# Zero-padded queries, DMA transposes of token-order q and k, W_tok copies moved to ScalarE and a longer lag of the channel product, in an attention-and-mixing kernel

**Chip, cores, metric.** One core of one Trainium2 chip. The metric is device time in microseconds (us), median over executions. A run is called slow when it took over 1.5% more than the fastest run of the same kernel; a profile is called slow when it was taken in such a run. Engines in the profile: PE (TensorE matmuls), PEld (its weight loads), DVE (VectorE), ACT (ScalarE), POOL (GpSimd), SP (SyncE, which here only issues DMAs).

## The reference

```python
# q, k, v: 4 batches, 8 heads, 768 tokens, 64; n_global = 8, n_local = 96
scores = q @ k^T / 8 + ALiBi bias; only the 8 first keys and the last 96 are kept
x = (softmax(scores) @ v), heads side by side          # 4 x 768 x 512
theta = x @ w_theta
y = w_tok_r @ (x * cos(theta)) + w_tok_i @ (x * sin(theta))   # over tokens
u = x + y
out = u + relu(u @ w_ch)
```

The inputs are drawn with a factor of 0.1, so scores are close to 0: a kernel that uses another batch's q or k stays within the tolerance of the comparison, one that uses another batch's v does not.

## The kernel before

Batch 0 is attended first; after that each batch's token mixing on PE is woven with the attention of the next. `b` is the batch, `p` a pair of heads. Four parts matter.

Loads go through GpSimd, in a layout where each partition holds six consecutive tokens (long runs), so that a copy on DVE and six PE transposes per operand are needed to get q and k transposed in token order:

```python
def load_qk(b, h0, n, which=(0, 1)):
    for i_ in which:
        nc.gpsimd.dma_start(out=qk[:, i_, h0:h0 + n].rearrange("p h t d -> p h (t d)"),
            in_=(q, k)[i_][b, h0:h0 + n].rearrange("h (p t) d -> p h (t d)", p=T))

def prep(b, p, w=0):
    ...
    with behind("dve"):            # L189: reorder, q and k
        for i_ in range(2):
            (nc.scalar.copy if b == 0 and i_ and p < 2 else nc.vector.tensor_copy)(
                out=qkn[:, :, i_]..., in_=qk[:, i_, 2 * p:2 * p + 2])
    for i_, dst in ((0, qT), (1, kT)):
        for t_ in range(NT):       # L198
            nc.tensor.transpose(ps[:, t_, :], qkn[:, t_, i_]..., ident)
        if i_ == 0:
            nc.vector.tensor_copy(out=dst, in_=src)      # L203
        else:
            nc.scalar.copy(out=dst, in_=src)             # L205
    nc.vector.tensor_copy(out=kG, in_=kT[...])           # L209
    nc.vector.tensor_copy(out=kG[:, :, 0:NG], in_=...)   # L210
```

The scores of the two heads of a pair are matmuls of 64 rows each (L230, `R = slice(D * hh, D * (hh + 1))`). The transposes of x (theta needs them) and, from batch 1 on, of u (the channel product needs them) are DMA transposes issued by SyncE:

```python
def xtrans(b, p, ...):   # L292
    nc.sync.dma_start_transpose(out=xT_sb[b][:, p, :]..., in_=x_sb[b][:, p]...)
def utrans(b, tt):
    nc.sync.dma_start_transpose(out=uT, in_=u)
def chan(b, tt):         # L357: the channel product, `lag` tiles behind the mixing
    nc.tensor.matmul(ps_c, lhsT=uT[:, dc, :], rhs=w_ch_bf[:, dc, :], ...)
```

And the order of a batch:

```python
for b in range(B):
    if b + 2 < B:
        load_all(b + 2)
    lag = 2
    ...   # rest of the channel products, prep of b + 1, theta of b
    ...   # mixing of b (and channel products) woven with attention of b + 1
```

The softmax here doesn't subtract the row's maximum and nothing guards it: scores larger than these inputs give would overflow.

## Time and profile before

| | before |
|---|---|
| median (3 runs) | 191.09 us (190.76 to 193.43) |
| profiled span | 189.6 us |
| PE busy | 89% of the span |
| DVE, ACT, POOL busy | 73%, 54%, 14% |

The first theta matmul of each batch is a mark. It cuts the run into stages: from theta of batch 0 to theta of 1 (the mixing of 0, the preparation of 1, the attention of 1), theta of 1 to theta of 2, theta of 2 to theta of 3, and the rest. The next lines are the kernel before, cut there: length, then busy time and count of PE, PEld, DVE, ACT, POOL; granted clock; DMA share; GB/s.

```profile
29.50:76.70 47.20, 44.31 (x465) 25.52 (x474) 38.74 (x87) 29.92 (x37) 6.49 (x4) 1.00 1.73 153
76.70:118.50 41.80, 38.02 (x337) 18.95 (x340) 31.01 (x66) 23.24 (x26) 1.75 (x2) 0.96 0.90 133
118.50:156.80 38.30, 36.69 (x339) 18.77 (x344) 31.45 (x67) 22.74 (x25) 0.00 (x0) 1.00 0.37 80
156.80:189.60 32.80, 27.63 (x127) 11.99 (x127) 14.05 (x26) 6.56 (x7) 0.00 (x0) 1.00 0.32 97
```

PE is busy for all but 3 us of the first stage and 4 us of the second. Stages two and three have the same work on PE; the second is 3.5 us longer, and its clock of 0.96 points to the reason: PE stood for a late uT and ran at half clock for a while afterwards (the prediction shows the wait).

### The profile page before, as it was taken

The page shows a single profiled execution, that of the slowest core. Times are in us where ns is not written, and L with a number is a line of the kernel's source. Part 1 is how long each engine was busy: PE and PEld are TensorE (multiplying, and loading weights), DVE is VectorE, ACT ScalarE, POOL GpSimd, SP SyncE. Part 2 cuts the span into 40 slices and gives each one's busy share as a digit, 9 for nine tenths or more (in the row PEclk, how much of TensorE's full clock was granted, in tenths as well). Part 3 has the DMA queues.
Part 4 walks back from the last instruction along what each step waited for, and adds up shares of the span by engine and source line. Part 5 has one row for each costly group of instructions (what it writes and reads, how often), then busy time and mean ns, then how long its engine had stood idle before and what let it go on. Part 6 is the DMA issues. An engine that isn't in the chain of part 4 may idle for free.

```text
span 189.6 us, 3693 instructions
## 1 busy us (share of the span) xinstructions
PE 167.9 (89%) x1500; PEld 89.1 (47%) x1523; DVE 137.9 (73%) x309; ACT 102.9 (54%) x122; POOL 27.1 (14%) x31
## 2 busy tenths in 40 slices
PE   7855787899999999999939999999999999999981
PEld 2424665445656555654414454644454544434430
DVE  5839987386999997998853786998877864734422
ACT  2469988871397684598724360499663604800010
POOL 7974361300040004020000000000000000000000
PEclk9999669999999999999987999999999999999999
DMA  4999999999999983999991337301165374113432
GB/s 63 153 188 181 210 209 207 204 189 142 130 83 182 225 116 75 148 142 146 223 116 58 74 91 185 109 3 55 28 66 141 88 145 148 59 32 107 118 106 111
DMA packets 58081, 23.97 MB, mean 126 GB/s; under 512 B 44240, under 2 KB 54992, under 8 KB 58064
## 3 DMA queue, kind: packets, MB, share of 16 engines
q0 software_dynamic: 35760, 12.85, 70.6%
q1 hardware_dynamic: 22304, 10.88, 25.0%
q8 instruction: 12, 0.20, 0.5%
q14 instruction: 5, 0.04, 0.1%
HBM read 25.69 MB, written 6.29 MB: 169 GB/s over the span
## 4 chain that ended last, share of the span: by engine, by line
PE 55%; ACT 14%; DVE 13%; DMA 12%; issue 2%; POOL 2%; ACTq 0%; POOLq 0%
PE ps L332 22%; PE ps L357 10%; DMA uT<-u 8%; PE pb L313 7%; ACT e L234 6%; PE pb L230 5%; DMA vn<-in_v_dram 4%; PE pb L278 4%; DVE qT L203 4%; ACT cs L317 3%; PE ps L198 3%; DVE qkn L189 2%; PE ps L278 2%; DVE zri L321 2%; POOL qk L72 2%
## 5 line engine op out<-in xcount | busy, mean ns | idle before, releaser
L234 ACT ACTIVATE e<-pb 128x1024 bf16<-128x1024 f32 (+1 forms) x48 | 44.1, 958 | 25.8 <-PE pb L230 25.7
L332 PE MATMUL ps<-zri,w_tokT_111 128*128 128x512 bf16 x141 | 53.6, 381 | 0.9 <-issue 0.3
L332 PE MATMUL ps<-zri,w_tokT_110 128*128 128x512 bf16 x130 | 49.5, 382 | 1.3 <-DVE zri L321 0.8
L337 DVE TENSOR_TENSOR u<-x_sb,ps 128x512 bf16<-128x512 bf16 x24 | 16.5, 687 | 16.6 <-PE ps L332 16.0
L357 PE MATMUL ps<-w_ch_bf,uT 128*128 128x512 bf16 x94 | 25.3, 391 | 3.7 <-DMA uT<-u 3.5
L360 DVE SCALAR_TENSOR_TENSOR o_sb<-ps,u 128x512 f32<-128x512 f32 x24 | 16.5, 687 | 11.4 <-PE ps L357 11.4
L313 PE MATMUL pb<-w_theta_bf,xT 128*128 128x512 bf16 x93 | 23.6, 379 | 0.7 <-ACT xT L299 0.4
L321 DVE TENSOR_TENSOR zri<-x_sb,cs 128x512 bf16<-128x512 bf16 x48 | 18.3, 421 | 7.2 <-ACT cs L317 6.1
L242 DVE TENSOR_TENSOR e<-e,etab 128x1024 bf16<-128x1024 bf16 (+1 forms) x32 | 19.7, 617 | 3.5 <-ACT e L234 3.5
L230 PE MATMUL pb<-qT,kT 64*128 64x128 bf16 x224 | 17.9, 231 | 4.7 <-ACT e L234 4.6
L332 PEld LDWEIGHTS <-w_tokT_110 128*128 128x128 bf16 x144 | 14.1, 98 | 15.2 <-issue 1.1
L332 PEld LDWEIGHTS <-w_tokT_111 128*128 128x128 bf16 x144 | 14.1, 98 | 13.2 <-issue 0.5
L205 ACT COPY kT<-ps 128x768 bf16<-128x768 bf16 x16 | 12.9, 805 | 13.4 <-PE ps L198 13.4
L230 PEld LDWEIGHTS <-kT 64*128 64x128 bf16 x224 | 10.0, 99 | 18.3 <-issue 16.7
L351 ACT COPY uT<-ps 128x512 bf16<-128x512 bf16 x7 | 4.1, 587 | 26.1 <-PE ps L350 26.1
L317 ACT ACTIVATE cs<-pb,halfpi 128x1024 bf16<-128x1024 f32 x12 | 13.4, 1120 | 8.9 <-issue 6.8
L278 PEld LDWEIGHTS <-e 128*128 128x128 bf16 x352 | 14.7, 100 | 6.8 <-issue 1.0
L198 PE MATMUL ps<-ident,qkn 128*128 128x128 bf16 x192 | 16.1, 232 | 1.1 <-DVE qkn L189 0.9
L198 PEld LDWEIGHTS <-qkn 128*128 128x128 bf16 x192 | 12.8, 103 | 8.4 <-DVE qkn L189 6.1
L230 PE MATMUL pb<-qT,kG 64*128 64x128 bf16 x128 | 13.6, 228 | 2.0 <-DVE kG L210 2.0
L203 DVE COPY qT<-ps 128x768 bf16<-128x768 bf16 x16 | 15.2, 947 | 0.0
L357 PEld LDWEIGHTS <-uT 128*128 128x128 bf16 x96 | 8.4, 99 | 13.5 <-DMA uT<-u 4.7
(63 smaller groups left out, 204.3 us busy)
## 6 DMA issues: line engine op xcount, KB each, us to landing
out_dram<-o_sb SPq DMA_DIRECT2D x24, 256.0 KB, 2.3
qk<-in_q_dram POOLq DMA_DIRECT2D x3, 768.0 KB, 8.1
qk<-in_k_dram POOLq DMA_DIRECT2D x3, 768.0 KB, 13.6
vn<-in_v_dram POOLq DMA_DIRECT2D x3, 768.0 KB, 22.7
w_nat<-in_moe_w_tok_r_dram POOLq DMA_DIRECT2D x3, 384.0 KB, 13.6
w_nat<-in_moe_w_tok_i_dram POOLq DMA_DIRECT2D x3, 384.0 KB, 14.8
qk<-in_q_dram POOLq DMA_DIRECT2D x4, 192.0 KB, 6.4
qk<-in_k_dram POOLq DMA_DIRECT2D x4, 192.0 KB, 6.7
```

What stands on the lines that cost most here:

```text
L198: nc.tensor.transpose(ps[:, t_, :], qkn[:, t_, i_].rearrange("p h d -> p (h d)"), ident)
L203: nc.vector.tensor_copy(out=dst, in_=src)
L230: nc.tensor.matmul(pb[:, hh, o:o + T], lhsT=lhsT, rhs=qT[R, (own, nxt)[part]], start=True, stop=True)
L234: ins = nc.scalar.activation(e_c, pb[:, :, 0:n], AF.Exp, scale=scale).ins
L242: nc.vector.tensor_mul(e_c, e_c, tab[:, :, s0:s0 + n // T].rearrange("p a s n -> p a (s n)"))
L278: nc.tensor.matmul(o, lhsT=l_, rhs=r_, start=(i_ == 0), stop=(i_ == len(mms) - 1))
L313: nc.tensor.matmul(pb[:, j, :], lhsT=xT[:, dc, st * T:(st + 1) * T], rhs=w_theta_bf[:, dc, :], start=(dc == 0), stop=(dc == NC - 1))
L317: nc.scalar.activation(cs[:, 0], pb, AF.Sin, bias=halfpi)
L321: nc.vector.tensor_mul(zri[b][:, i_, 2 * c + j_, :].rearrange("p (g d) -> p g d", g=NP), xb[:, :, 2 * c + j_, :], cs[:, i_, j_].rearrange( ...
L332: anchor["pe"] = nc.tensor.matmul(ps, lhsT=w_tokT[wi][:, st, tt * T:(tt + 1) * T], rhs=zri[b][:, wi, st, :], start=(st == 0 and wi == 0), ...
L337: anchor["dve"] = nc.vector.tensor_add(u_sb[b, tt].rearrange("p (g d) -> p g d", g=NP), x_sb[b][:, :, tt, :], ps.rearrange("p (g d) -> p g ...
L357: nc.tensor.matmul(ps_c, lhsT=uT[:, dc, :], rhs=w_ch_bf[:, dc, :], start=(dc == 0), stop=(dc == NC - 1))
```

## The change

The intent: PE and DVE are full, the DMA engines and GpSimd are not. So (1) q and k of batches 2 and 3 are loaded in token order and transposed by DMA, which frees 48 PE transposes and some 16 copies a batch; (2) since such a transpose brings two heads or a head and zeros at once, q is kept zero-padded (`qZ`: 128 rows, the other head's are 0), and the scores of batches 1 to 3 use all 128 rows; (3) SyncE's order is fixed to the program's; (4) W_tok copies go from DVE to ScalarE; (5) the channel product comes three tiles behind the mixing instead of two in batches 1 to 3. The small constants move into other buffers to make room.

```diff
+    def load_qk_nat(b):
+        if b == 2:
+            for a in range(2):
+                nc.gpsimd.memset(q_nat[:, a::2, :, 1 - a, :], 0.0)
+        for h in range(H):
+            for i_, dst in ((0, q_nat[:, h, :, h % 2, :]), (1, k_nat[:, h // 2, :, h % 2, :])):
+                nc.gpsimd.dma_start(out=dst, in_=(q, k)[i_][b, h].rearrange("(t p) d -> p t d", p=T))
...
-            (copy if wi else nc.vector.tensor_copy)(out=w_tokT[wi][:, :, tt * T:(tt + 1) * T], in_=ps)
+            nc.scalar.copy(out=w_tokT[wi][:, :, tt * T:(tt + 1) * T], in_=ps)
...
+        if b > 1:
+            with behind("pe"):
+                for dst, src in ((kT, k_nat[:, p]), (qT[:, 0], q_nat[:, 2 * p]), (qT[:, 1], q_nat[:, 2 * p + 1])):
+                    nc.sync.dma_start_transpose(out=..., in_=...)
+            return
...
+            if i_ == 0 and b:
+                for hh, copy in ((0, nc.scalar.copy), (1, nc.vector.tensor_copy)):
+                    R = slice(D * hh, D * (hh + 1))
+                    copy(out=dst[R, hh]..., in_=src[R])
+                continue
...
-                    R = slice(D * hh, D * (hh + 1))
+                    R = slice(0, T) if b else slice(D * hh, D * (hh + 1))
...
-        lag = 2
+            lag = 3 if b else 2
...
-            order = rest[:-1] + pre[:2] + th[:2] + pre[2:] + th[2:3] + rest[-1:] + th[3:]
+            order = pre + rest[:-1] + th[:3] + rest[-1:] + th[3:] + keys[:1]
```

(`keys[:1]` is the kG copy of the first pair. The natural buffer `home` shares its space with batch 1's run layout, so batch 2's q waits for batch 1's reorder copies, and each load of batch 3 for the transpose that frees its part. Cut: buffers, constants, SyncE's manual order.)

## The prediction

> **What bounds the kernel now.** I read the page's slices first, then the busy time of each engine by stage, then the chain of waits, then single lines. The slices show TensorE (PE) nearly full from slice 8 on; slice 21 (99.5 to 104.3 us) is the only late one with a lowered clock.
>
> ```profile
> PE   7855787899999999999939999999999999999981
> PEclk9999669999999999999987999999999999999999
> DMA  4999999999999983999991337301165374113432
> ```
>
> I cut the time after batch 0's attention where the chain changes from mixing (L332) to the transposes and theta (L198, L313) and back. Columns: length, then busy time and count of PE, weight loads, DVE, ACT, GpSimd (POOL), clock, DMA.
>
> ```profile
> 42.00:75.40 33.40, 32.41 (x366) 19.17 (x373) 29.77 (x64) 19.54 (x24) 4.17 (x3) 1.00 1.92 136
> 75.40:88.00 12.60, 12.50 (x103) 6.58 (x104) 12.31 (x34) 9.56 (x12) 1.86 (x3) 1.00 1.38 141
> 88.00:118.80 30.80, 27.13 (x248) 13.10 (x252) 20.30 (x36) 13.77 (x15) 0.00 (x0) 0.94 0.69 131
> 118.80:130.00 11.20, 10.97 (x90) 5.91 (x91) 11.09 (x31) 8.80 (x10) 0.00 (x0) 1.00 0.19 61
> 130.00:155.30 25.30, 24.27 (x245) 12.46 (x248) 19.37 (x34) 13.94 (x16) 0.00 (x0) 1.00 0.42 82
> ```
>
> I call them B (mixing of batch 0 beside attention of 1), C (theta of 1, preparation of 2), D (mixing of 1, attention of 2), E and F (the same one batch on), G the rest. In B and in C and E, DVE is as full as PE; D and F are PE's own. D is 5.5 us longer than F with the same work, and the chain says why: a transposed u came late behind the loads of batch 3.
>
> ```profile
> 90.08 8.61 DMA uT<-u
> 98.69 0.05 issue
> 98.74 1.89 PE ps L357 x4
> ```
>
> PE stood 3.1 us (95.6 to 98.7), and the 3.4 us after that ran at a granted clock of 0.54, so about 1.6 us more were lost.
>
> Durations that I need, from the groups by form and the per-tile view:
>
> ```profile
> L205 ACT COPY kT<-ps 128x768 bf16<-128x768 bf16 x16 | 12.9, 805 | 13.4 <-PE ps L198 13.4
> L203 DVE COPY qT<-ps 128x768 bf16<-128x768 bf16 x16 | 15.2, 947 | 0.0
> L162 DVE COPY w_tokT_110<-ps 128x768 bf16<-128x768 bf16 x6 | 3.3, 554 | 2.4 <-PE ps L161 2.4
> L292 SPq DMA_TRANSPOSE xT<-x_sb x12: 1209/1214/1889, 63.1 to 154.4; - x12
> DMA to landing us min/median/max: 2.7/2.8/6.3
> 83.39 0.85 PE ps L198 x12
> 125.96 0.69 PE ps L198 x12
> ```
>
> PE's true pitch is in the last two: 12 transposes in 0.69 us, 57.5 ns each, when nothing holds them.
>
> The score matmuls, from the timeline of PE (start, busy time):
>
> ```profile
> 102.63 0.19 PE L278 MATMUL pb<-vG,e 128*128 128x65 bf16 x1
> 102.76 0.23 PE L230 MATMUL pb<-qT,kT 64*128 64x128 bf16 x2
> 102.83 0.22 PE L230 MATMUL pb<-qT,kG 64*128 64x128 bf16 x2
> ...
> 102.94 0.22 PE L230 MATMUL pb<-qT,kG 64*128 64x128 bf16 x2
> 103.09 0.39 PE L332 MATMUL ps<-zri,w_tokT_110 128*128 128x512 bf16 x1
> ```
>
> **What the Trainium skill says.** (1) "TensorE: Matmul & The Clock Gate", Part 1: a warm matmul of 128 columns starts every 55.6 ns, one of 512 every 215.7 ns, and an idle array falls to half clock. The trace agrees: 57.5 ns, 0.216 us from one L332 start to the next, and the 0.54 clock after the gap. (2) "TensorEngine Tiling (Array Packing)", Key Properties: a change of tiling mode drains the array. The trace agrees: the eight 64-row score matmuls that begin at 102.76 follow each other by 57 ns per pair of heads, but 0.10 us is lost before them and 0.09 us after them; 0.43 us in all. (3) "DMA: Bandwidth & Descriptors", Queues, rings and completion order: each DMA engine goes round its queues a packet at a time. So a load and a transpose share: the same uT transpose lands 2.4 us after issue at the median and 8.6 us at worst, in the load of batch 3.
>
> **Zero-padded scores.** Batches 1 to 3 use all 128 rows, one matmul per head: a group of 8 costs 8 x 57.5 ns = 0.46 us against 0.43 with the drains; a group of 6, 0.35 against 0.37. A batch has 8 groups of 8 and 4 of 6: +0.2 us a batch. That is a wash, not a gain. What it buys is that the transposed DMA of zero-filled q needs no shuffle.
>
> **Transposes by DMA (batches 2, 3).** C and E each lose 48 PE transposes (48 x 57.5 ns = 2.8 us), 8 qkn copies on DVE (8 x 0.35 = 2.8), 4 qT copies (3.8) and, on ACT, 4 kT copies (3.2). Added on SyncE: 12 transposes of 128x768 at 1.21 us of issue, 14.5 us a batch. The theta stage does not shrink by all 2.8: six Sin of about 1.07 us (6.4) and a table load (1.28) follow the first theta in series. With two chans and four theta pieces ahead of it the first Sin begins some 3.5 us in, as it does now; I take 0.8 us of new PE idling. So -2.0 for each of C and E.
>
> Does the data arrive? Natural-order loads are runs of 64 instead of 384 elements. From the DMA table in 58 to 62 us the long runs went at 266 packets/us, so q and k of one batch (2048) take 7.7 us; v's short ones (79 to 81) at 1134 per us, so 12288 would take 10.8. GpSimd's issue was 0.73 us for 2 rows per partition and 1.46 for 24: about 0.85 us for 6, so 16 issues take 13.6 us. For batch 2, k needs no buffer of the run layout and comes early; q must wait for the qkn copies (L189, to 54 us) and should land by about 70, before the transposes at about 76. Good.
>
> For batch 2 the transposes run from the end of B, beside v of batch 3 (6144 short packets, 5.4 us) and then k and q of batch 3, which follow pair by pair as the transposes release the natural buffer. Work for the DMA engines from there: 12 x 0.93 us (768 packets at some 830 per us, an estimate from the transposes at 116 to 118 us) + 5.4 + 10.8 = 27 us; so the last pair may come 26 us after the start, and SyncE's fixed order puts the uT of D behind it. The first chan of D wants its uT about 24 us after the start (lag is now 3 tiles). I put a loss of 2.7 us between 0 and 5.5. For batch 3 no load runs and 14.5 us of issue fits before the uT is wanted.
>
> **D and F otherwise.** The 3.1 us stand and 1.6 us half-clock of D go: -4.7, with +2.7 new and +0.2 for padding. F: +0.2. The longer lag moves one chan out of D into E and one out of F into G, which is no gain in itself.
>
> **B.** Ten W_tok copies leave DVE there (10 x 0.55 = -5.5 us) and go to ACT at 0.8 (the duration of its copies from PSUM), +8. The q eviction of batch 1 is now two half copies, each still 768 elements long (L259 on 128 partitions takes 0.70 us and L260 on 8 takes 0.69, so partitions do not count): DVE keeps 4 x 0.95, ACT gains 4 x 0.8 = 3.2. ACT goes from 19.5 to 30.7 us in a stage of 33.4. Its exponentials can start only after q, k and W_tok copies, 2 to 4 us later than the present 54.2. PE's work does not shrink in B. I take +1.8. The zero fills on GpSimd sit behind a DMA backlog that lasts to 53 us, so cost nothing.
>
> **G.** The wait of 0.7 us for a uT of batch 2 (PE at 155.2 to 155.95) goes: -0.7. The 1.2 us hole at 182.5, before the last u's transposes, stays, since PE's built order still has those transposes ahead of the last chans.
>
> Sum: B +1.8, C -2.0, D -1.8, E -2.0, F +0.2, G -0.7 = -4.5, giving 186.6. My D figure may be harsh, since the lag was lengthened for exactly this wait and the DVE relief in B is real; I take 1.4 us off for that and say 185.2.
>
> **Rivals.** *DMA takes over in D.* If transposes are served only after the natural loads, the first uT comes 5 to 8 us late, PE falls to half clock again and D gains nothing: 189 to 191. For it: the 8.6 us landing, and each load now in four times as many packets. Against: the loads of batch 3 themselves wait for the transposes, so cannot run ahead. *ACT becomes B's bound.* 30.7 busy of 33.4 with waits between gives +4: 187.5. For it: ACT row above; against: back-to-back ACT copies start 0.7 us apart, not 0.8. *All hidden.* Transposes finish under theta and mixing; B unchanged: 180 to 181. For it: DMA is under half used after 100 us.
>
> **Range and chances.** The first two rivals add, the third takes off as much: 180 to 190.5. Faster by over 2% is below 187.3, with the centre 2 us under it: 0.68. Within 2%: 0.28. Slower than 194.9 needs both bad rivals at once: 0.04.
>
> **What would show it.** Right: no L198 work after B, C about 10.5 us, ACT above 28 us in B with the first exponential at 56 to 58, D's wait on uT no longer than 5 us, kT and qZ transposes of the second preparation at 2.8 us landing and the first at 5 or more. Wrong: an idle PE of over 5 us waiting for uT or qZ in D, a DVE that waits for kT with the zri products behind it, or B longer than 38 us. If D falls by 6 us or more the DMA sharing was far milder than I took.

## The result

| | before | after |
|---|---|---|
| median | 192.2 us (4 runs, 190.76 to 193.43) | 206.28 us (4 runs, 204.49 to 208.65) |
| profiled span | 189.6 | 206.6 (a slow run) |
| PE, DVE, ACT, POOL busy | 89, 73, 54, 14% | 84, 64, 52, 28% |

The changed kernel is slower: ratio 1.065, 95% interval 1.049 to 1.082. A ratio here and below is the mean time of one kernel's fast runs over that of the other's of the same rounds, so not quite the ratio of the quoted medians. The profiled run of after was one of its slow ones; its fast runs were 204.5 and 204.9 us. So I read only waits from it that a fast profile of a variant shows too (the variant of experiment 1 has the same ones, most of them shorter, at 204.5 us of span).

The slices of after (40 of 5.2 us), to set against those in the prediction:

```profile
PE   6856878899669999983899289979997998999982
PEclk9999589999757999997599969999999999999998
DMA  5999999999999137599999992777788567305424
```

PE has holes at slices 10, 18 and 22 (52, 93 and 114 us), each with a lowered clock at or after it, and DMA is full from slice 17 to 23 and at 0.7 to 0.8 from 25 to 30, where before it was mostly at 0.3 or less from slice 21 on. By stage, after:

```profile
30.00:85.30 55.30, 49.15 (x467) 30.24 (x464) 40.08 (x75) 39.98 (x51) 21.31 (x21) 0.91 1.49 131
85.30:135.20 49.90, 39.56 (x300) 21.13 (x298) 26.92 (x54) 20.74 (x22) 13.69 (x17) 0.90 1.48 146
135.20:173.40 38.20, 35.21 (x297) 19.17 (x296) 26.57 (x55) 19.84 (x21) 0.00 (x0) 1.00 0.73 152
173.40:206.60 33.20, 27.76 (x129) 12.06 (x127) 14.12 (x27) 6.56 (x7) 0.00 (x0) 0.97 0.37 102
```

Of the 17 us between the two profiles, 8.1 are in the first stage, where POOL works 21.3 us instead of 6.5, and 8.1 in the second. About 4 of the 17 belong to the slow run (208.65 against 204.5 and 204.9); in which stage they fell is not known. The third, without its 48 PE transposes, is only 0.1 us shorter, though PE's busy time there is 1.5 us less and DVE's 4.9. PE's waits in it (in all, times, longest), which before had one of 0.4 us for a uT:

```profile
PE pb L354 <- DMA xT<-x_sb: 1.4, 1, 1.4
PE ps L398 <- DMA uT<-u: 1.2, 1, 1.2
```

**The first stage.** One of DVE's copies in the kernel before (start, busy time); then DVE's timeline of after, and GpSimd's over the same time:

```profile
49.93 0.17 DVE L210 COPY kG<-kT 128x32 bf16<-128x32 bf16 x1
```

```profile
51.31 2.10 DVE L207 COPY kG<-kT 128x32 bf16<-128x32 bf16 x1
55.25 2.73 DVE L207 COPY kG<-kT 128x32 bf16<-128x32 bf16 x1
```

```profile
51.22 2.21 POOL L90 DMA_DIRECT2D vn<-in_v_dram  x1
...
54.87 1.70 POOL L86 DMA_DIRECT2D home<-in_q_dram  x2
56.55 1.40 POOL L83 MEMSET home<- 128x1536 bf16 x1
```

A copy of 32 columns took 0.17 us in the kernel before; here one takes 2.10 and ends at 53.41 us with GpSimd's issue of v (53.43), another 2.73, beside two issues of q and a zero fill, and ends at 57.98 just after the fill (57.95; GpSimd's ends are rough in this profile). The Trainium skill has the mechanism, in "SBUF — State Buffer", Who interferes with whom: DVE in a two-port mode (which copies can enter if their operands allow it) and GpSimd share a pair of ports under an exclusive lock, and the second to come blocks wholly. The trace agrees by the ends above; the experiments test it. This is what I did not think of. Why GpSimd is busy then: in before, v of batch 2 was issued at 32.5 us, long before; in after its issue (51.2) stands behind the keys' eight small loads, the last five of which wait for earlier transfers to land.

**The second stage.** DVE's timeline of after (in brackets: idle before, and what ended it), then the chain of waits:

```profile
85.23 0.69 DVE L401 SCALAR_TENSOR_TENSOR o_sb<-ps,u 128x512 f32<-128x512 f32 x1 [0.18 <-PE ps L398]
94.72 0.29 DVE L206 COPY kG<-kT 128x512 bf16<-128x512 bf16 x1 [8.80 <-DMA kT<-home]
95.13 0.76 DVE L362 TENSOR_TENSOR zri<-x_sb,cs 128x512 bf16<-128x512 bf16 x2
```

```profile
88.75 10.17 DMA qZ<-home
...
110.69 8.62 DMA uT<-u
119.31 0.05 issue
119.36 1.71 PE ps L398 x4
```

DVE stood 8.8 us for the first transposed keys of batch 2, with the zri products that the mixing of batch 1 needs queued behind; then the uT of the channel product took 8.6 us, behind the 12 transposes and beside the loads of batch 3. The 8.6 us that bounded this stage in before are still there, though the product is wanted a tile later, and the 8.8 are new. GpSimd issues loads in this stage too, but they hold DVE little: no kG copy there takes over 0.58 us.

### The profile page after: what moved, and what is told of

Read it like the earlier page. It is cut to its first block, busy times and chain, and to the rows that moved or that the text cites.

```text
span 206.6 us, 3598 instructions
## 1 busy us (share of the span) xinstructions
PE 173.5 (84%) x1427; PEld 96.4 (47%) x1427; DVE 132.5 (64%) x274; ACT 107.8 (52%) x129; POOL 58.7 (28%) x69
## 4 chain that ended last, share of the span: by engine, by line
PE 47%; DVE 20%; DMA 17%; ACT 7%; SPq 4%; issue 2%; POOL 1%; ACTq 0%; POOLq 0%
PE ps L373 23%; PE ps L398 7%; PE pb L272 6%; DMA uT<-u 6%; DMA qZ<-home 5%; DMA vn<-in_v_dram 4%; PE pb L354 3%; PE pb L319 3%; DVE kG L207 3%; DVE e L283 2%; ACT cs L358 2%; ACT e L275 2%; DVE e L286 2%; DVE zri L362 2%; POOL home L76 1%
## 5 line engine op out<-in xcount | busy, mean ns | idle before, releaser
L373 PE MATMUL ps<-zri,w_tokT 128*128 128x512 bf16 x288 | 77.4, 394 | 5.4 <-DVE zri L362 5.3
L275 ACT ACTIVATE e<-pb 128x1024 bf16<-128x1024 f32 (+1 forms) x48 | 44.3, 959 | 31.5 <-PE pb L272 31.5
L373 PEld LDWEIGHTS <-w_tokT 128*128 128x128 bf16 x288 | 26.9, 101 | 30.9 <-issue 8.8
L272 PEld LDWEIGHTS <-kT 128*128 128x128 bf16 (+1 forms) x224 | 17.4, 106 | 15.4 <-issue 11.3
L272 PE MATMUL pb<-qZ,kT 128*128 128x128 bf16 x168 | 19.7, 232 | 0.9 <-DMA qZ<-home 0.5
L86 POOL DMA_DIRECT2D home<-in_k_dram x16 | 13.3, 836 | 23.0 <-DMA kT<-home 9.5
L86 POOL DMA_DIRECT2D home<-in_q_dram x16 | 13.6, 858 | 8.0 <-DMA qZ<-home 7.7
L354 PEld LDWEIGHTS <-xT 128*128 128x128 bf16 x96 | 8.8, 98 | 14.8 <-DMA xT<-x_sb 4.4
L90 POOL DMA_DIRECT2D vn<-in_v_dram x5 | 9.6, 1923 | 20.5 <-DVE rec L327 20.4
L272 PE MATMUL pb<-qZ,kG 128*128 128x128 bf16 x96 | 13.6, 232 | 0.2 <-DVE kG L207 0.2
L319 PE MATMUL pb<-vn,e 128*128 128x65 bf16 x168 | 12.3, 193 | 0.6 <-DVE e L286 0.4
## 6 DMA issues: line engine op xcount, KB each, us to landing
w_nat<-in_moe_w_tok_i_dram POOLq DMA_DIRECT2D x3, 384.0 KB, 14.3
```

The lines of the kernel that those rows point to most:

```text
L86: nc.gpsimd.dma_start(out=dst, in_=(q, k)[i_][b, h].rearrange("(t p) d -> p t d", p=T))
L272: nc.tensor.matmul(pb[:, hh, o:o + T], lhsT=lhsT, rhs=rhs, start=True, stop=True)
L275: ins = nc.scalar.activation(e_c, pb[:, :, 0:n], AF.Exp, scale=scale).ins
L319: nc.tensor.matmul(o, lhsT=l_, rhs=r_, start=(i_ == 0), stop=(i_ == len(mms) - 1))
L354: nc.tensor.matmul(pb[:, j, :], lhsT=xT[:, dc, st * T:(st + 1) * T], rhs=w_theta_bf[:, dc, :], start=(dc == 0), stop=(dc == NC - 1))
L373: anchor["pe"] = nc.tensor.matmul(ps, lhsT=w_tokT[wi][:, st, tt * T:(tt + 1) * T], rhs=zri[b][:, wi, st, :], start=(st == 0 and wi == 0), ...
```

## The experiments

All times below are medians; "stages" are the four lengths between the theta marks in the one profile of that run. The jobs ran on different chips, each with its own runs of before; in the job of 9 to 12 two runs of before took 326 us, for a reason not known, and count as slow.

| kernel | us | ratio to before | stages |
|---|---|---|---|
| before | 191.8 to 192.5 | 1 | 47.2, 41.8, 38.3, 32.8 |
| after (slow profile) | 206.28 | 1.065 | 55.3, 49.9, 38.2, 33.2 |
| 1 after, W_tok on DVE | 207.47 | 1.078 | 51.2, 49.2, 40.8, 33.2 |
| 2 after, batch 2 loaded later | 208.30 | 1.082 | 49.0, 54.8, 38.4, 33.2 |
| 3 after, batch 3 loaded later | 200.29 | 1.044 | 50.5, 42.6, 40.9, 33.2 |
| 4 before, zero-padded q | 191.43 | 0.998 | 50.3, 37.4, 39.0, 32.7 |
| 5 before, lag 3 | 185.71 | 0.976 | 47.2, 38.1, 37.2, 32.4 |
| 6 before, GpSimd fills (slow profile) | 194.33 | 1.021 | 50.6, 42.1, 38.4, 32.7 |
| 7 after, no loads of batch 3 | 193.37 | 1.012 | 54.4, 36.8, 37.8, 33.1 |
| 8 after, kG behind zri (slow profile) | 205.98 | 1.079 | 54.2, 50.4, 40.4, 33.2 |
| 9 before, lag 3, W_tok on ACT | 190.47 | 0.996 | 48.0, 41.9, 37.2, 32.4 |
| 10 after, no v of batch 3 (slow profile) | 198.64 | 1.037 | 54.5, 44.3, 38.8, 33.1 |
| 11 after, no q, k of batch 3 (slow profile) | 199.16 | 1.043 | 53.9, 43.8, 38.8, 34.1 |
| 12 after, loads of 2 and 3 all gone | 187.81 | 0.985 | 48.4, 35.6, 38.3, 33.1 |
| 13 after, no zero fills | 202.87 | 1.060 | 50.9, 47.5, 38.6, 33.2 |
| 14 as 13, v of batch 2 first | 203.20 | 1.059 | 49.1, 49.3, 40.6, 33.2 |

My theory after the traces: GpSimd's memory work in the first stage holds DVE's copies, and in the second the short-packet loads delay the DMA transposes. Rivals: ScalarE's extra copies are the first stage's loss; the fixed order of SyncE, or of DVE, is the second's.

### 1. W_tok copies back on DVE

```diff
-            nc.scalar.copy(out=w_tokT[wi]..., in_=ps)
+            (copy if wi else nc.vector.tensor_copy)(out=w_tokT[wi]..., in_=ps)
```

> The changed kernel with only the W_tok copies as before (all but one on DVE). In the changed kernel the first exponential of batch 1 starts at 63.2 us instead of 54.2, and two DVE key copies (kG, 0.2 us each as a rule) take 2.1 and 2.7 us there, each ending to the hundredth with a GpSimd instruction (the v load's issue, a memset). Theory 1, GpSimd's issues and memsets block DVE's copies: W_tok copies are not the cause, the first theta of batch 1 stays at 83 to 88 us (85.3 in the changed kernel, 76.7 before), total within 3 us of the changed kernel's 204.5 to 208.7. Theory 2, ScalarE became the bound of the stage as I had feared: the stage shortens by 3 us or more and the total falls to 202 or less.

207.47 us. The first stage is 4 us shorter than in after's slow profile, but no shorter than in experiment 3, which leaves W_tok on ScalarE (50.5), so nothing here says that the copies are what after lost. The whole is no faster: in this fast profile DVE again waited 7.5 us for the keys of batch 2, and one kG copy took 1.18 us where 0.29 is normal. (The same code of the first stage took 50.5 and 54.4 us in the fast profiles of 3 and 7, so a difference of 4 us in this stage between two single profiles proves little.)

### 2 and 3. The loads held back

A dependency holds batch 2's loads and fills until the first exponential of batch 1 (2), or batch 3's loads until the twelfth transpose of batch 2 has landed (3).

```diff
+                more = [lambda: load_all(2, lambda: exps[1, 0, 0])]          # experiment 2
...
-            more = [lambda b=b: load_all(b + 2)] if b + 2 < B else []
+            more = [lambda b=b: load_all(b + 2, (lambda: hops[11]) if b else (lambda: None))] if b + 2 < B else []   # 3
```

> The changed kernel with GpSimd's k, q, v loads and memsets of batch 2 made to wait for the first exponential of batch 1, so that no GpSimd work lies in batch 1's preparation. Theory 1 (GpSimd blocks DVE): no kG copy over 0.7 us in the preparation, first exponential of batch 1 at 54 to 57 us, first theta of batch 1 at 77 to 80 us, total down by 5 to 9 us. Theory 2 (ScalarE's W_tok and q copies hold the stage): first exponential stays over 60 us, total the same. A risk for both: batch 2's loads now come 25 us later, so its transposes may start late and give part of it back behind theta of 1.

> The changed kernel with all loads of batch 3 held until the twelfth transpose of batch 2 has landed. Theory 3 (natural loads beside the transposes make kT of batch 2 late: it landed 9 us after its issue, and DVE stood 8.8 us before the kG copy with the zri products behind it): kT lands in under 4 us, DVE waits under 1.5 us, theta of batch 1 to theta of batch 2 (49.9 us in the changed kernel, 41.8 before) falls to 41 to 44 us, total down 5 to 9 us. Rival (twelve transposes in fixed SyncE order are too slow by themselves): DVE still waits over 3 us or uT is late by over 4 us, that stretch stays over 47 us.

Experiment 2: 208.30 us. With GpSimd quiet in the preparation of batch 1 the kG copies take their 0.17 and 0.29 us and the first stage drops to 49.0 (the first exponential comes at 58.6, later than the 54 to 57 expected); but the loads that were put off now run into the transposes of x and of batch 2, PE waits 8.0 us for one uT, and the second stage grows to 54.8. Experiment 3: 200.29 us, the best form of the whole change. The second stage falls to 42.6 us, as the theory said; the loads then meet the keys of batch 3 (DVE stood 7.9 us for them) and the third stage grows to 40.9. Both say the same: the wait moves with the loads.

### 4 and 5. Parts alone on the kernel before

```diff
+                    R = slice(0, T) if b else slice(D * hh, D * (hh + 1))    # 4: zero-padded q, half copies
...
-        lag = 2
+        lag = 3 if b else 2                                                  # 5 (u, uT: one buffer more)
```

> The kernel before with zero-padded queries alone in batches 1 to 3 (TensorE transposes kept, q evicted in two halves by ScalarE and DVE, run-layout loads, small constants moved into output buffers to make room). My prediction's step 'a wash': PE's score groups 0.46 us of 8 instead of 0.43, total 190.5 to 194, within 1% of before. Rival (padding has a price, by 12 more ScalarE copies of 0.8 us and twice the columns streamed): 195 or more. Rival (mode changes cost more than I counted): 188 or less.

> The kernel before with the channel product three tiles behind the mixing in batches 1 to 3 (with the larger u and uT buffers), nothing else of the change. Theory: the uT that came late behind the load of batch 3 is wanted later, so the 3.1 us stand of PE and its half clock go: theta of 1 to theta of 2 falls from 41.7 to 37.5-38.5 us and the time to 187-188.5 (ratio 0.975-0.985). Rival: the load is met somewhere else (xT, or the next chan), the stand moves: 191-192, ratio 0.995-1.00.

Zero-padding alone: 191.43 us, ratio 0.998 (0.995 to 1.001), a wash. But not because it costs nothing: the first stage is 3.1 us longer, and the first exponential of batch 1 comes at 57.5 us instead of 54.2 (ScalarE now has four half copies of q besides, 0.79 us each; that these are the reason is argued, not shown); the second stage is 4.4 us shorter, and PE waits for no uT in it.

The second stage of before, and with the lag alone:

```profile
76.70:118.50 41.80, 38.02 (x337) 18.95 (x340) 31.01 (x66) 23.24 (x26) 1.75 (x2) 0.96 0.90 133
75.80:113.90 38.10, 37.54 (x354) 19.07 (x352) 31.74 (x68) 23.25 (x26) 1.75 (x2) 1.00 0.97 144
```

The lag alone: 185.71 us, ratio 0.976 (0.965 to 0.988). It is the fastest version found, and the only part of the change that gained when tried by itself (the DMA transposes were never tried without the rest). It takes 3.7 us out of the second stage and no wait for a uT is left in it. The prediction had called this part "no gain in itself".

### 6. GpSimd's work by itself

```diff
+    def fills(to):
+        for _ in range(10):
+            ins = nc.gpsimd.memset(scratch, 0.0).ins   # 128x768, unused; held by batch 1's first reorder copy
```

> The kernel before with ten fills of an unused 128x768 tile on GpSimd, started by the first reordering copy of batch 1's keys: GpSimd has 8 us of memory work inside the preparation of batch 1 and no data depends on it. Theory (copies of DVE stand while GpSimd writes memory or descriptors): several bf16 copies of DVE between 47 and 56 us (kG, qkn, normally 0.17 to 0.36 us) take 0.7 us or more, the first exponential of batch 1 comes 1.5-4 us later than 54.2, the first theta of batch 1 at 78.5-81 instead of 76.7, the time 193-196. Rival (the long copies of the changed kernel have another cause, such as their PSUM source or the order): the copies keep 0.17-0.36 us and the time stays within 191-192.5.

194.33 us, ratio 1.021 (1.009 to 1.032) in fast runs. The first line is GpSimd's, the rest are DVE's, in this run's (slow) profile:

```profile
49.37 8.58 POOL L177 MEMSET scratch<- 128x768 bf16 x10 [12.94 <-DVE qkn L196]
```

```profile
51.25 0.90 DVE L196 COPY qkn<-qk 128x768 bf16<-128x768 bf16 x1
52.07 0.90 DVE L218 COPY kG<-kT 128x512 bf16<-128x512 bf16 x1
53.56 0.94 DVE L212 COPY qT<-ps 128x768 bf16<-128x768 bf16 x1
```

The copies from SBUF to SBUF take about the length of a fill, 0.90 instead of 0.35 (qkn) and 0.29 (kG); the copy from PSUM keeps its 0.94 us. So only the first kind was held here. With nothing depending on the fills, the first stage is 3.4 us longer in the slow profile, and the fast runs are 2.1% longer as a whole. That GpSimd's work holds these copies is so shown, not only argued. The other profiles agree: in the preparation of batch 1 (45 to 62 us) no kG or qkn copy takes over 0.5 us in before, 2, 4, 5 and 12, where GpSimd does little then; in after, 1, 3, 7, 8, 10, 11 and 13 the longest takes 0.92 to 2.73.

### 7 to 9. No loads; DVE's order; ScalarE alone

```diff
+        if b == 3: loads[3] = loads[1]; return                     # 7, in load_all: wrong on purpose
...
-        with behind("dve") if b > 1 else nullcontext():            # 8: first kG behind the last zri product
+        with behind("zri") if b > 1 and p == 0 else behind("dve") if b > 1 else nullcontext():
...
-            (copy if wi else nc.vector.tensor_copy)(out=w_tokT[wi]..., in_=ps)   # 9, on experiment 5
+            nc.scalar.copy(out=w_tokT[wi]..., in_=ps)
```

> The changed kernel without the loads of batch 3: its scores and values use batch 2's queries and keys and batch 1's v, so batch 3 of the result is wrong on purpose; all transposes, matmuls and copies stay. Theory (the transposes are late because they share with the natural-order loads): keys of batch 2 land 2.8-3.5 us after issue, DVE stands under 3 us for the first, theta of 1 to theta of 2 takes 41-43.5 us instead of 49.9, theta of 2 on as in the changed kernel (71), the stage of mixing 0 as there (81-85 to theta of 1): 194-199 in all. Rival (the fixed SyncE order and 12 transposes in a row are late by themselves): theta of 1 to theta of 2 stays at 47 us or more, time 203-207.

> The changed kernel with the first kG of batches 2 and 3 behind the last zri product on DVE, and those after it in turn; the transposes come as late as before. Theory (DVE's order makes a late key transpose stop mixing as well): the 8.8 us stand of DVE goes, PE mixes meanwhile, theta of 1 to theta of 2 falls by 3-6 us from 49.9, time 200-203. Rival (only the lateness matters, PE would run out of mixing and wait for the scores): falls by under 2 us, 204-207.

> The kernel with only the longer lag (the one that ran at 185.7), and all W_tok copies on ScalarE as in the change. Theory (the prediction's ScalarE term for the mixing of 0, +1.8 us, was too high: the one experiment that gave the copies back to DVE gained nothing): theta of batch 1 at 75-77 us against 75.8, the time 184.5-187 (ratio to before 0.97-0.98). Rival (exponentials wait for ScalarE's copies): first exponential of batch 1 2 us or more after 53.3, theta of 1 at 77.5-80, the time 187.5-190.

Experiment 7 (its result is wrong): the second stage falls from 49.9 to 36.8 us, further than I expected, the key transposes land in 2.8 us, and SyncE's order is the same. So neither that order nor the 12 transposes in a row are the loss; the loads are. The landing of the key transposes (after, from 80 to 100 us; then 7, from 78 to 130):

```profile
DMA to landing us min/median/max: 6.2/9.1/10.2
DMA to landing us min/median/max: 2.7/2.8/2.8
```

Experiment 8: 205.98 us and a second stage of 50.4 (slow profile), as the rival had it: with the zri products ahead, PE's waits only have another name. Its waits between 80 and 136 us:

```profile
PE pb L272 <- DMA qZ<-home: 5.4, 2, 3.3
PE ps L398 <- DMA uT<-u: 5.4, 2, 5.2
```

So DVE's order is not the cause either; the lateness is.

Experiment 9 fell out against my theory: 190.47 us (20 runs), where the lag alone had 185.71 in another job; ratios to before 0.996 and 0.976. The exponentials start 4.2 us later (57.5), the last x of batch 1 is transposed later, and just after the first theta matmuls PE stands 2.4 us for an xT, with a half clock after it (0.50 from 82 to 84 us). The theta mark comes before that wait, so the stage before it shows only 0.8 us and the next one 3.8.

```profile
PE pb L313 <- DMA xT<-x_sb: 2.4, 1, 2.4
```

Where GpSimd does not hold DVE, moving W_tok to ScalarE costs about 4 us (0.996 - 0.976 of 192; the two intervals, 0.993 to 1.000 and 0.965 to 0.988, do not meet).

### 10 to 12. Which load does what, and what is left without any

```diff
+        if b == 3: loads[3] = loads[1]; load_qk_nat(b); return     # 10: no v of batch 3
...
-        if b > 1: load_qk_nat(b)
+        if b == 2: load_qk_nat(b)                                  # 11: no q, k of batch 3
...
-        if b > 1: load_qk_nat(b)                                   # 12: no q, k of 2 and 3, no v of 3, no fills
```

(The cuts run lines together; 12 also fills the key buffer with zeros once, at the start.)

> The changed kernel without the load of batch 3's v alone (batch 3 computes with another batch's v: wrong on purpose); q and k of batch 3 are still loaded pair by pair behind the transposes. Theory (v's 6144 packets hold the first transposes, q's and k's hold the uT): the first key transpose of batch 2 lands in 3-4 us, DVE stands under 3.5 us for it, but the uT of batch 1 still comes late; theta of 1 to theta of 2 42-46 us (49.9 in the changed kernel, 36.8 without q, k and v), time 198-202. Rival (q and k do all of it): 48 us or more, 204-207.

> The changed kernel without the loads of batch 3's q and k (batch 3 uses batch 2's: wrong on purpose); v of batch 3 is still loaded. Theory as for its twin without v: the first key transpose stays late (8 us or more to landing) and DVE stands 6-9 us for it, the uT comes in time; theta of 1 to theta of 2 41-45 us, time 197-201. Rival (v does no harm): 36.5-39 us, 192-195, as without all three.

> The changed kernel without the natural-order loads and fills of batches 2 and 3 and without v of batch 3 (wrong on purpose): what the change would be if its loads cost nothing. Theory (loads and GpSimd's work are the whole loss, and the removed transposes and copies gain almost nothing beyond the longer lag): to theta of 1 49-51 us from the first theta, then 36.5-38, then 37.5-39, 33; time 185.5-188.5, not faster than the lag alone (185.7). Rival (the transposes by DMA do gain once nothing disturbs them): 180-183.

The waits in the second stage of 10 (PE's, then DVE's for the first keys) and of 11, each as a sum, a count and the longest:

```profile
PE ps L398 <- DMA uT<-u: 5.1, 1, 5.1
...
DVE kG L206 <- DMA kT<-home: 6.7, 2, 4.3
```

```profile
PE ps L373 <- DVE zri L362: 4.1, 2, 3.2
...
DVE kG L206 <- DMA kT<-home: 12.8, 2, 8.7
```

Without v, DVE's wait for the first keys is 2.3 us (the 4.3 are for batch 3's, later) and the uT stays late; without q and k, no uT wait is left, and the keys stay 8.7 us late. Each is worth about 6 us (44.3 and 43.8 against 49.9), both together 13. These profiles, after's included, fell in slow runs. The fast runs' ratios (1.037 and 1.043, against 1.065 with all loads and 1.012 with none of batch 3's) put the two at about 5 and 4 us of the whole time and both together at 10. The split in waits rests on the slow profiles.

Experiment 12 is the bound: with all natural-order loads and fills gone, 187.81 us. The first stage is 1.2 us longer than before's, the second 6.2 shorter, the third the same. Had the loads been free, the change would gain 1.5% (0.3 to 2.7), no more than its lag alone gains (2.4%, 1.2 to 3.5). The second stage of 12:

```profile
78.40:114.00 35.60, 35.16 (x301) 19.13 (x299) 26.50 (x54) 20.44 (x22) 0.00 (x0) 1.00 0.77 137
```

This does not say that the transposes gain nothing. 12 still has W_tok on ScalarE, and experiment 9, with the lag and that move, stood at 0.996 in the same job; so padding and transposes with free loads may be worth about 1% (the intervals overlap). No run has the lag and the transposes with W_tok left on DVE and the loads free, so what they could give there is open.

### 13 and 14. What in the first stage holds DVE

These two runs were for the one open point: fills, or the issue of loads.

```diff
-            for a in range(2):                                     # 13, 14
-                nc.gpsimd.memset(q_nat[:, a::2, :, 1 - a, :], 0.0)
...
+        if b == 2: load_v(b, 0, 8); load_qk_nat(b); return         # 14 alone
```

> The changed kernel without the zero fills of the natural-order query buffer (other heads' queries stay in its other halves: batches 2 and 3 wrong on purpose); loads, transposes and matmuls as they are. Theory (the fills are what holds DVE during the preparation of batch 1): first theta to theta of batch 1 falls to 49-51 us (50.5 to 55.4 in kernels with the fills), time 200-203. Rival (the issues of the loads hold DVE just as well, v's of 2.2 us first of all): 52-55 us, one kG or qkn copy of 1.5 us or more beside the issue of v; time 204-207.

> As the run without fills, with v of batch 2 loaded ahead of its queries and keys, so that its 2.2 us of issue lie before the preparation of batch 1; some of the keys' loads come later instead. If v's issue holds DVE: first theta to theta of batch 1 at 48.5-50.5 us and 1.5-4 us less than without fills alone. If any issue does: 51-55 us as there. The stages after it stay as in the changed kernel (49-50 us, then 38-41), so the time is 199-204 or 203-207.

Without the fills the first stage takes 50.9 us, and one copy is still long, beside v's issue (DVE, then GpSimd):

```profile
50.81 1.72 DVE L203 COPY kG<-kT 128x512 bf16<-128x512 bf16 x1
```

```profile
50.19 2.22 POOL L87 DMA_DIRECT2D vn<-in_v_dram  x1
```

With v ahead as well no kG or qkn copy takes over 0.50 us, and the stage takes 49.1. So an issue holds DVE as the fills of experiment 6 do. What each is worth is less sure: the issue of v 1.8 us by these two profiles, the fills anything up to 3.6 (kernels with them ran from 50.5 to 54.5 in this stage, after's slow profile aside, against 50.9). In 14 the time is not better than in 13, since keys that are loaded later delay the second and third stage: the wait moved again.

## Why the prediction was wrong

Predicted 185.2 us, measured 206.28, outside the range, and the wrong way. The steps that failed are two: that GpSimd's work costs nothing in B, and that sharing DMA with the loads costs 2.7 us in D. My stages B, D and F end within 2 us of the theta marks, and B begins later (42.0 us against 29.5), so the comparison is rough by that much. By its steps:

- **B, +1.8.** Measured +8.1 in the first stage, and 4.0, 3.3 and 7.2 in the fast profiles of experiments 1, 3 and 7, which keep all of batch 2's loads and fills there. The step that failed is "the zero fills on GpSimd sit behind a DMA backlog that lasts to 53 us, so cost nothing": from 51 to 58 us they and the loads' issues hold DVE's copies (6, 13, 14). Without them there the stage is +1.2 (12) or +1.8 (2), close to the +1.8 for ScalarE and padding. That agreement is partly luck: alone, padding lengthened this stage by 3.1 (4), and W_tok by 0.8 with 3.8 more in the next (9); these do not add up to it, and why is not known.
- **C and D, -3.8.** Measured +8.1. Without the sharing my sum was -6.5 (-2.0, -4.7, +0.2); without the loads of 2 and 3 the runs show -6.2 (12). So the gain was sized right in sum (its parts less so: in this stage the lag alone gave -3.7, padding alone -4.4, and W_tok took 3.8), and the term that failed is the sharing: "a loss of 2.7 us between 0 and 5.5", in fact 49.9 - 35.6 = 14.3 us (49.2 - 35.6 = 13.6 with experiment 1's fast profile). I sized it for one transfer, the uT. The runs show two: v of batch 3 delays the first keys (11), q and k delay the uT (10). The rival "DMA takes over in D" was argued away with "the loads of batch 3 themselves wait for the transposes, so cannot run ahead". That holds for q and k and not for v, whose buffer came free with the end of batch 1's attention: it was issued at 83.6 us, ahead of the first transpose at 85.6.
- **What the skill's packet rule was worth.** In the prediction I cited from "DMA: Bandwidth & Descriptors" that DMA engines serve their queues in turn, packet by packet. I drew from it that the loads and the transposes share. The first key transpose's landing grew from 2.8 us to 9.1, more than an even split of the engines' time would give by itself; the runs do not show how the packets alternate.
- **E and F, -1.8.** Measured -0.1, and 0.0 in 12, which has no loads there. PE's work did fall; "I take 0.8 us of new PE idling" failed: PE waited 1.4 us for an xT and 1.2 for a uT, 2.6 in all, in the profile of after and, with the same numbers, in that of 12. That the 48 transposes had been filling such waits (before had one of 0.4 us) is argued, not shown.
- **G, -0.7.** Measured +0.4. The wait of 0.7 us that I took off lies just before the mark. After it PE waits 0.6 us for an xT, in after and in 12 (33.2 and 33.1 us), and not in before (32.8) nor with the lag alone (32.4).
- **"The longer lag ... is no gain in itself."** Wrong, and the largest error of attribution: I credited the vanishing of D's stand and half clock (-4.7) to the change as a whole. The lag alone has it (5: -3.7 in this stage, 2.4% in time).
- **Padding "a wash".** Right in time (4), though not by PE's arithmetic alone.
- **What would show it wrong** was well chosen: DVE waiting for kT with the zri products behind it, and B longer than 38 us. The first exponential came at 63.1 in the slow profile and at 59.6 to 61.3 in the fast ones of 1, 3 and 7, not 56 to 58. One small misreading: not only slice 21 but also slice 20 has a lowered clock (0.8), as the line shown there says. The chances (0.04 for slower) were too sure: the losses in B and in D have a common source, the finer loads, and no rival of mine had it for B.

What stays open: the size of a single stall in the first stage varies from kernel to kernel (50.5 to 54.5 us of stage), and I cannot say from these runs which order of instructions gives which; why padding alone lengthens it by 3.1 us; and what the transposes would give with the lag alone.

## What to carry to other kernels

Moving work off a full engine onto DMA did not pay here because the loads that feed it became dearer: count packets and GpSimd's issues, and ask of each buffer when it is free, since that sets when its load runs and what it meets. GpSimd's fills and DMA issues were not free beside DVE copies from SBUF to SBUF (0.17 us became up to 2.73); put them where DVE does something else. And try each part of a change alone: here the smallest one, a channel product one tile later, was the only one that gained by itself.

## What the Trainium skill lacked or had wrong

- "SBUF — State Buffer": its warning box on GpSimd's DMAs tells only of DVE holding up the writing of descriptors. Here it is the other way: one issue of 2.2 us (v, 128x48x64) held a copy of 0.17 us for 2.10, and two issues of q with a fill of 1.40 held one for 2.73. The page's general rule (the second to come blocks) covers it, the box does not.
- "DMA: Bandwidth & Descriptors", Queues, rings and completion order: it gives the turn-taking by packets, but no size for what a load of short packets does to a transpose. Here a 128x768 transpose landed in 2.8 us without batch 3's loads, in 9.1 beside v's; a 128x512 one in 2.4 and 8.6.
- I found no page on how long SyncE's issue of a DMA transpose lasts when the DMA engines are loaded: 1.21 us at the median, 5.02 for one key transpose here.
